# Mirrored row blocks of 16 instead of 32 in a linear-attention and Fourier-mixing kernel, with a new written-out order of work

## The chip, the cores and the metric

The kernel runs on one core of one Trainium2 chip. The metric is the device time of one execution in microseconds (us): 415.05, the median of 3 runs (414.36, 415.05 and 419.71). The core's engines have names in what follows: PE is the matrix engine (PEld is its weight load), DVE the vector engine, ACT the scalar engine, POOL the engine GpSimd, and SP issues transfers. POOL and ACT issue transfers too. Each engine works through its own queue strictly in the order in which the program put the instructions there, and waits at an instruction until what it needs is ready.

## The reference

```python
def phi(x):
    proj = np.einsum('bhsd,df->bhsf', x, w_phi)
    proj = proj - np.max(np.abs(proj), axis=-1, keepdims=True)
    return np.concatenate([np.exp(proj), np.exp(-proj)], axis=-1)
q_p, k_p = phi(q), phi(k)
kv = np.einsum('bhsf,bhsd->bhfd', k_p, v)
z = np.sum(k_p, axis=2)
num = np.einsum('bhsf,bhfd->bhsd', q_p, kv)
den = np.einsum('bhsf,bhf->bhs', q_p, z)[..., None] + 1e-06
x = (num / den).transpose(0, 2, 1, 3).reshape(B, S, H * D)

u = x + np.real(np.fft.fft(np.fft.fft(x, axis=1), axis=2))
un = (u - mean(u)) / np.sqrt(var(u) + 1e-06)
out = u + np.maximum(un @ w_ch1, 0.0) @ w_ch2
```

There are 8 batches, 8 heads, 576 rows and 64 columns a head, so x is 576 x 512 in each batch. The feature width of phi is 128, the hidden width of the last line 2048. All inputs and the output are float32; the kernel multiplies in bfloat16.

## The kernel before, in words

Each batch goes through four stages. (1) *Attention*: the features of k and q are projected by PE (psk L468, psq L522, psh L563), put through exp by ACT (KPp, KPn, QPHP, QPHN), their largest values are taken by DVE (MK L488, MQ L530), and v is scaled with them by POOL (VCn and VCp, L443). Then PE multiplies per head kv (L853, L857) and pn (L955), DVE combines the two halves (tg, cb, rd) and POOL writes x for two heads at a time into the tile X (L975). (2) *Mixing*: the two Fourier transforms are matrix products on folded rows. DVE folds X into R (L869 to L893, L998) and into CEO (L1007, L1053), PE multiplies with the tables SS and CS (psD L1035; L1019 in batch 0) and with CD and SD (pu L1087), and DVE adds the result to X (L1077). (3) *Normalising*: DVE measures each chunk of 128 rows (L1157, L1158), ACT writes UN (L1133), and a transpose by the transfer engines, issued by SP, makes UT (L1150). (4) *Feed-forward*: PE multiplies UT with W1 into psf (L1207, function `hidden`), ACT writes HT, PE multiplies with W2 into pso (L1224, `output(c)`; L1250 and L1270 for the rest), DVE adds into X (L1230), and `store` sends the chunk to the output.

Row n and row 576-n of a real transform mirror each other, so the 576 rows lie in X in five chunks: chunks 0 and 1 hold rows 1 to 256 in pairs (two neighbouring rows in one partition), chunks 2 and 3 the mirrored rows 320 to 575, chunk 4 the other 64. For the fold, the mirror image of a row must lie in the same partition. That is reached by blocks: before the change, rows 1 to 256 are cut into 4 blocks of 32 partitions in falling order (`193 - 64 * a`), and the mirrored chunk is read backwards within each block of 32 (`rearrange("p h (a r) -> p (h a) r", r=32)[:, :, ::-1]` in `queries`, a `stream_shuffle` with the mask 31 to 0 in `weigh_q`, and `rows_[:, ::-1, ...]` in the store). So q is loaded for rows 1 to 256 by 4 transfers, and chunks 0 and 1, which are stored together as "chunk 1", by 4 stores.

The order of the work is written out by hand in the string `PLAN`. Each letter advances one stream by one step: T, P, R and S are parts of attention, M mixing, D the fold, N normalising, U the scales, F the feed-forward, K, V and Q issue loads on POOL, A and B issue the transposes of q and k on SP, and Y is a *stir*: four matmuls without use that keep PE running in the start (L1322, psum tile `idle`). A step puts its instructions at once into the queues of all engines that it uses. The streams of several batches are interleaved, so that PE works on the feed-forward of batch b while the other engines prepare batch b+1.

Loads of k, v and q are issued by POOL (L258) among its own arithmetic; the stores and the transposes by SP, in one queue. In the last batch some stores are issued by ACT.

Of the kernel before, what the change touches and what calls it, by code (L numbers as in the profile page):

```python
# [10 lines left out]
ALU = mybir.AluOpType  # L11
AX = mybir.AxisListType
F32 = mybir.dt.float32
# [10 lines left out]
    "CYCCZYCYGGTRTTGZZGTYZWRTJTSRJGRJYSTPTSPKTTPJMJRTSSKMYMBMPTQPTPQVTMZTMQTMMTPCMMMTTMTHDYAMMYHHDHHKYYVD"  # L24
    "YDTMTMHTKZMRMSRTYMTTMNYMRVTYQNNMTNTSMNMBFFFRFFNUFNFSMFWFUNRUFQUMTPSFFMNTFPSMTFTNUPYFQMUFPPTVMFTPMTPF"
    "FMMFTTFMFAUTFMMFFMFMFMFMFFKRFPDFFTTTFFDVFFDRFTFFVDFFKTSRFQVFFFFMFFMTFRFFFFFSMTMFFMRTFFMSTMFTFNNMFMQF"
    "PTMMFTFSFMPTFFPTTPMFFFFMFSNBFMFPTQMFFAFMNPFTFMNMFFMFFMMFTTFFURMFFVFRMFFSTFFMFFMFVFTTPFFFFRFPDFFFTPFF"
    "FFFVDDRFFFQFDTMTFFQTSMKFFFMFFFKMRMFTTTMMFNNFFMMFMQFMFFSSMTFMTFFFNFSTPPMFTFMBFPTFPAMFFFMFNTFKMMFFFNFM"
    "FMFFMFFUMQMFFVMFFFTTPFFFFMTFFRFTTFFVFFFRFFRFDFFFFDFDFFDPTFMFTTFFFFMKFRFTMSFMRFFMFTSPMFNTMPQNSFFFFQMM"
    "MMTTTFFBMSFFFFTPMTFSFFMFFMTPVMFFFFMTPNFFNNMMMFFMAFFFMUFMFKMFFFMFFTTDTTFRFFSFFFFRVFFTMFFFFFRPTFFDFFFD"  # L30
    "RFFFTDFMFVKTPFFFFFMTMBQMFFRSFMFTSTSTMMKFFFNNSFMMFMMFTFMFPTMKFFFFPTPMTFFMFFFNMFTPPMFFFTNFQMNMVFFMFQMF"
    "MFFMUFFMFFVMAFFFFTTTTFDRFRFFTFSFFFFMRFFQFFFDFFTFFFDFFRFVDFTFMFFTTMFFMFFMFRSMFQTTTMFTQFNFMSVFFMFFTNPM"
    "MFMSTPMTFFFFSMTPPMFTFFMPPFBAFMFPFMFNNFMMVFMFMFFFMTTFRMNUFFFFFMRFFFMFFFSTFFMFFPTFFTFFFDDFFFRFTFFFDFDV"
    "RFFFMFTTFFMFMTMFRFFSMFFSFMTTNTFFMFNMMFFFMMFTFMPSTFNFFFPTFMFFTMPFFFFMPSPMFFTMFFPFTMNFFFNMFMFFFUMFMFMF"
    "FFFMFFMFMFFFFFDFFDFFFFFDFFFDFMFFFMFMFFMMFFMFNFMNFFFFFFMFFFFFMNFFFMFFNFFFFFFFFFFFFFFFNUFFFFFFFFFFFFFF"
# [5 lines left out]
def kernel(  # L41
# [74 lines left out]
    rc, rs = gc[:, 0:C], ga[:, 3 * NK:4 * NK]  # L116
    pc = const.tile([128, 5], F32, name="pc")
# [25 lines left out]
    def count_first():  # L143
        for a in range(4):
            count(pc[32 * a:32 * a + 32, 0:2], [[1, 2]], 193 - 64 * a, 2)
        count(pc[:, 2:3], [[1, 1]], 256, 1)
        nc.gpsimd.memset(pc[0:1, 2:3], 0.0)
        for j in range(2):
            count(
                rs[:, 128 * j:128 * j + 128].rearrange("p (a r) -> p a r", r=32),  # L150
                [[-64, 4], [2, 32]], 193 + j, 0,
            )
# [21 lines left out]
    def constants(b):  # L174
        nc.vector.tensor_scalar_mul(out=pn[:, 0:3], in0=pc[:, 0:3], scalar1=1.0 / S)
# [91 lines left out]
    def make_q(b):  # L267
# [138 lines left out]
    def features(b):  # L406
# [195 lines left out]
    def first_features():  # L602
# [21 lines left out]
        def project(ps, t, outer, last):  # L624
            for x, pr in enumerate((0, 3) if outer else (1, 2)):
                for jj in range(2):
                    rr = slice(64 * jj, 64 * jj + 64)
                    rq = (QT01, QT23)[t][rr, 2 * pr:2 * pr + 2, :]
                    rq = rq.rearrange("p h (a r) -> p h a r", r=32)
# [25 lines left out]
        def negative(t, outer):  # L655
            ps = pj.tile([128, 2, 4, 128], F32, tag="pj", name="psn")
            project(ps, t, outer, False)
            m = rows_of_m[outer][:].rearrange("p (a r) -> p a r", r=32)
# [521 lines left out]
    def store(b, U, c):  # L1180
        if c == 1:
            for a in range(4):
                queue = nc.scalar if b == B - 1 and a % 2 else nc.sync
                queue.dma_start(
                    out=out[b, 193 - 64 * a:257 - 64 * a, :].rearrange("(r j) n -> r j n", j=2),
                    in_=U[32 * a:32 * a + 32, 0:2, 0:C],
                )
        elif c in (2, 3):
            rows_ = out[b, 320:576, :].rearrange("(a r j) n -> a r j n", r=32, j=2)
# [201 lines left out]
```

## Time and profile before

| what | value |
|---|---|
| runs | 414.36, 415.05, 419.71 us |
| the profiled execution: its own time, its span | 415.15 us, 413.4 us |
| granted PE clock, mean | 0.995 |
| busy PE, PEld, DVE, ACT, POOL | 394.6, 259.5, 319.4, 303.8, 215.1 us |
| transferred | 42.71 MB |
| chain that ended last, by engine | PE 69%, DVE 13%, DMA 8%, ACT 4%, POOL 3%, issue 2% |
| largest parts of that chain | psf L1207 29%, pso L1224 19%, UT transposes 4% |

The span runs from the first to the last instruction. A row of the profile in order of time gives start, length, engine, line, operation, what is written and what is read, how many instructions were merged, and in brackets how long the engine stood idle before it and what ended that. A row such as "A L1 <- B L2: 2.8, 4, 1.3" in the list of waits says that A at line 1 waited for B at line 2 for 2.8 us in all, 4 times, at most 1.3. A row "580/605/1346" gives the shortest, the median and the longest duration in ns. A length in such rows includes the time in a pipeline, so two PE rows may overlap.

### The profile page before, as it was taken

What the parts mean: (1) busy time and instruction counts of PE and PEld (TensorE: products, weight loads), DVE (VectorE), ACT (ScalarE), POOL (GpSimd) and SP (SyncE); (2) the same over time, 40 slices, a digit from 0 to 9 for tenths busy, and PEclk for the clock granted to TensorE, in tenths of its full rate; (3) what the DMA queues carried; (4) which work ended last, traced back from release to release, by engine and by line L of the source; (5) the groups of instructions that cost most, each with busy time, mean ns of one, the idle gap of its engine ahead of it and who ended that gap; (6) DMA issues with size and microseconds to landing.
All of it is one profiled execution on the core that took longest, in us unless ns stands there. A gap on an engine that the chain in (4) does not pass through costs nothing.

```text
span 413.4 us, 10526 instructions
## 1 busy us (share of the span) xinstructions
PE 394.6 (95%) x4194; PEld 259.5 (63%) x4194; DVE 319.4 (77%) x662; ACT 303.8 (73%) x617; POOL 215.1 (52%) x279
## 2 busy tenths in 40 slices
PE   7898999989999989999899999999999999999994
PEld 3574577535856568566756577566856586658563
DVE  5979887999699867797689878888799768875101
ACT  6988999658958886688868886789758885544350
POOL 8997695774466753707658373649271343201000
PEclk9999899999999999999999999999999999999999
DMA  7999979898674899654965979757952141106103
GB/s 210 221 170 158 181 100 185 87 118 128 102 118 58 67 179 141 63 92 83 129 97 65 156 104 142 80 72 116 117 97 52 46 83 21 27 14 114 24 23 90
DMA packets 108520, 42.71 MB, mean 103 GB/s; under 512 B 82615, under 2 KB 103479, under 8 KB 108471
## 3 DMA queue, kind: packets, MB, share of 16 engines
q0 software_dynamic: 46272, 16.60, 37.1%
q1 hardware_dynamic: 61703, 24.85, 32.9%
q10 hardware_dynamic: 496, 0.59, 0.6%
q8 instruction: 33, 0.54, 0.5%
q14 instruction: 16, 0.13, 0.1%
HBM read 36.77 MB, written 9.44 MB: 112 GB/s over the span
## 4 chain that ended last, share of the span: by engine, by line
PE 69%; DVE 13%; DMA 8%; ACT 4%; POOL 3%; issue 2%; DVEq 0%; POOLq 0%; SPq 0%; ACTq 0%
PE psf L1207 29%; PE pso L1224 19%; DMA UT<-UN 4%; PE kv L853 3%; PE psD L1035 2%; PE psk L468 2%; DMA KT<-KS 2%; PE pu L1087 2%; DMA KS<-in_k_dram 2%; PE psq L522 2%; PE psh L563 1%; DVE MK L488 1%; PE pso L1250 1%; DVE cb L969 1%; DVE X L1077 1%
## 5 line engine op out<-in xcount | busy, mean ns | idle before, releaser
L1207 PE MATMUL psf<-UT,W1b 128*128 128x320 bf16 (+1 forms) x1024 | 141.1, 286 | 2.9 <-DMA UT<-UN 2.8
L1224 PE MATMUL pso<-W2b,HT 128*128 128x512 bf16 x496 | 120.5, 379 | 0.0
L1207 PEld LDWEIGHTS <-W1b 128*128 128x128 bf16 x1024 | 94.6, 98 | 30.9 <-issue 3.8
L1212 ACT ACTIVATE HT<-psf 128x320 bf16<-128x320 f32 x128 | 53.9, 444 | 25.7 <-PE psf L1207 19.5
L1224 PEld LDWEIGHTS <-HT 128*128 128x128 bf16 x496 | 45.2, 98 | 43.2 <-issue 0.4
L975 POOL TENSOR_TENSOR X<-cb,rd 128x640 f32<-128x640 f32 x28 | 35.1, 1254 | 52.9 <-DVE rd L973 29.6
L443 POOL TENSOR_TENSOR VCn<-VS,VCn 128x512 bf16<-128x512 bf16 x28 | 29.9, 1067 | 43.4 <-ACT VCn L438 36.6
L530 DVE TENSOR_REDUCE MQ<-psq 128x8 f32<-128x1024 f32 (+1 forms) x32 | 34.3, 1088 | 17.8 <-PE psq L522 17.4
L1230 DVE SCALAR_TENSOR_TENSOR X<-pso,rs,X 128x512 f32<-128x512 f32 x31 | 23.0, 743 | 28.2 <-PE pso L1224 28.0
L1214 ACT ACTIVATE HT<-psf 128x512 bf16<-128x512 f32 x64 | 37.3, 602 | 6.8 <-PE psf L1207 6.6
L488 DVE TENSOR_REDUCE MK<-psk 128x8 f32<-128x1024 f32 x28 | 33.8, 1210 | 1.4 <-ACT KPn L474 1.4
L474 ACT ACTIVATE KPp<-psk 128x1024 bf16<-128x1024 f32 x28 | 28.8, 1027 | 7.8 <-PE psk L468 7.5
L258 POOL DMA_DIRECT2D QS<-in_q_dram x49 | 33.4, 688 | 1.1 <-issue 1.1
L1133 ACT ACTIVATE UN<-X,MV 128x512 bf16<-128x512 f32 (+1 forms) x35 | 25.2, 726 | 11.5 <-DVE MV L1158 8.0
L572 ACT ACTIVATE QPHP<-psh 128x1024 bf16<-128x1024 f32 x28 | 28.9, 1031 | 4.8 <-PE psh L563 4.5
L474 ACT ACTIVATE KPn<-psk 128x1024 bf16<-128x1024 f32 x28 | 28.7, 1025 | 1.7 <-DVE MK L488 1.6
L443 POOL TENSOR_TENSOR VCp<-VS,VCp 128x512 bf16<-128x512 bf16 x28 | 29.9, 1067 | 0.0
L572 ACT ACTIVATE QPHN<-psh 128x1024 bf16<-128x1024 f32 x28 | 29.0, 1036 | 0.0
L1157 DVE BATCH_NORM_STATS2 st<-X 128x6 f32<-128x512 f32 (+1 forms) x40 | 27.1, 678 | 0.2
L1077 DVE TENSOR_TENSOR X<-pu,X 128x512 f32<-128x512 f32 (+3 forms) x49 | 23.5, 526 | 4.6 <-PE pu L1087 4.5
L955 PEld LDWEIGHTS <-QPHP 128*128 128x128 bf16 x280 | 20.5, 99 | 7.8 <-DVE cb L969 3.8
L1173 POOL TENSOR_TENSOR rs<-VE,mhalf 128x5 f32<-128x5 f32 (+1 forms) x9 | 10.3, 1148 | 24.8 <-DVE VE L1172 24.7
(462 smaller groups left out, 797.2 us busy)
## 6 DMA issues: line engine op xcount, KB each, us to landing
out_dram<-X SPq DMA_DIRECT2D x31, 128.0 KB
out_dram<-X SPq DMA_DIRECT2D x15, 256.0 KB
KS<-in_k_dram POOLq DMA_DIRECT2D x7, 512.0 KB, 8.2
VS<-in_v_dram POOLq DMA_DIRECT2D x14, 256.0 KB, 4.8
W1b<-in_moe_w_ch_dram POOLq DMA_DIRECT2D x1, 2048.0 KB, 15.3
W2b<-in_moe_w_ch_dram POOLq DMA_DIRECT2D x1, 2048.0 KB, 16.1
QS<-in_q_dram POOLq DMA_DIRECT2D x28, 64.0 KB, 3.6
QS<-in_q_dram POOLq DMA_DIRECT2D x7, 256.0 KB, 5.6
```

The source lines that it names most:

```text
L258: nc.gpsimd.dma_start(out=pieces[i][0], in_=pieces[i][1])
L443: nc.gpsimd.tensor_tensor(out=VC[:, hs, :, 0:D], in0=values[b][0][:, hs, :].rearrange("p h (j d) -> p h j d", d=D), in1=VC[:, hs, :, D:D + ...
L474: nc.scalar.activation(out=KP[:, hs, :, :].rearrange("p e (jp jj) f -> p jj (e jp) f", jj=2), in_=psk[:], func=AT.Exp, scale=sgn,)
L488: nc.vector.tensor_reduce(out=MK[:, 2 * pr:2 * pr + 2, :].rearrange("p e (jp jj) -> p jj (e jp)", jj=2), in_=tiles[pr][:], axis=AX.X, op=A ...
L530: nc.vector.tensor_reduce(out=o, in_=i[:], axis=AX.X, op=ALU.max, apply_absolute_value=True)
L572: nc.scalar.activation(out=o, in_=psh[:], func=AT.Exp, scale=sgn)
L975: nc.gpsimd.tensor_tensor(out=X[:, :, at:at + 2 * D].rearrange("p c (e d) -> p e c d", e=2), in0=cb[:, :, :, 0:D], in1=rd[:].to_broadcast( ...
L1077: nc.vector.tensor_tensor(out=to, in0=more, in1=to, op=ALU.add)
L1207: nc.tensor.matmul(ps, lhsT=W1b[:, cc, 128 * hh:128 * hh + 128], rhs=UT[:, cc, lo:hi], start=(cc == 0), stop=(cc == NCC - 1),)
L1212: nc.scalar.activation(out=HT[:, hh, lo:hi], in_=ps, func=AT.Relu, scale=-1.0)
L1214: nc.scalar.activation(out=HT[:, hh - 1:hh + 1, lo:hi], in_=psw[:].rearrange("p (a n) -> p a n", a=2), func=AT.Relu, scale=-1.0,)
L1224: nc.tensor.matmul(po[:], lhsT=HT[:, hh, at:at + 128], rhs=W2b[:, hh, :], start=(hh == 0), stop=(hh == NHH - 1),)
```

## The change

The blocks have 16 partitions instead of 32. So the q rows 1 to 256 of batches 1 to 7 are loaded by 8 transfers instead of 4, each half as large (the profile lists 64 KB for one of the 4), the stores of chunk 1 are 8 instead of 4, and the stores of the mirrored chunks have 8 blocks of 16 rows instead of 4 of 32. The backward reads work in blocks of 16, and the shuffle mask becomes `i ^ 15`. The tables of row numbers are made another way: two iotas fewer on POOL, three tiny steps more on DVE (a shift, a cast and a multiply-add). `PLAN` is another string: the same 1237 steps in another order. The matmuls, exponentials and reductions are the same in number and size. Most lines of the changed kernel have numbers that are 10 higher.

```diff
 PLAN = (
-    "CYCCZYCYGGTRTTGZZGTYZWRTJTSRJGRJYSTPTSPKTTPJMJRTSSKMYMBMPTQPTPQVTMZTMQTMMTPCMMMTTMTHDYAMMYHHDHHKYYVD"
+    "CZYGGTCGGCZRZZTCTWTJKSRYTPRJTSZTGYPJTSRPTJZRYMKMTSTYSJVPPTTPTQMMMTTQMMQVCTMPMMTBMTMTDKMHMYDHHHYYYYAD"
...
     def count_first():
-        for a in range(4):
-            count(pc[32 * a:32 * a + 32, 0:2], [[1, 2]], 193 - 64 * a, 2)
+        count(pc_i[:, 0:1], [[1, 1]], 0, 1)
+        count(pc[:, 0:2], [[1, 2]], 225, 2)
...
     def constants(b):
+        nc.vector.tensor_single_scalar(
+            out=pc_i[:, 1:2], in_=pc_i[:, 0:1], scalar=4, op=ALU.arith_shift_right
+        )
+        nc.vector.tensor_copy(out=blk[:], in_=pc_i[:, 1:2])
+        nc.vector.scalar_tensor_tensor(
+            out=pc[:, 0:2], in0=blk[:].to_broadcast([128, 2]), scalar=-64.0,
+            in1=pc[:, 0:2], op0=ALU.mult, op1=ALU.add,
+        )
...
-            (QS[:], q[b, :, at:at + 64 * n, :].rearrange("h (p j) d -> p h (j d)", j=2))
+            (QS[:], q[b, :, at:at + 32 * n, :].rearrange("h (p j) d -> p h (j d)", j=2))
             for QS, at, n in [
-                (QS01[32 * a:32 * a + 32], 193 - 64 * a, 1) for a in range(4)
-            ] + [(QS23, 320, 4)]
+                (QS01[16 * a:16 * a + 16], 225 - 32 * a, 1) for a in range(8)
+            ] + [(QS23, 320, 8)]
...
-                out=mq[:, hs, 2:4], in_=mq[:, hs, 2:4], mask=list(range(31, -1, -1))
+                out=mq[:, hs, 2:4], in_=mq[:, hs, 2:4], mask=[i ^ 15 for i in range(32)]
...
-                    rq = rq.rearrange("p h (a r) -> p (h a) r", r=32)[:, :, ::-1]
+                    rq = rq.rearrange("p h (a r) -> p (h a) r", r=16)[:, :, ::-1]
...
     def store(b, U, c):
         if c == 1:
-            for a in range(4):
+            for a in range(8):
                 queue = nc.scalar if b == B - 1 and a % 2 else nc.sync
                 queue.dma_start(
-                    out=out[b, 193 - 64 * a:257 - 64 * a, :].rearrange("(r j) n -> r j n", j=2),
-                    in_=U[32 * a:32 * a + 32, 0:2, 0:C],
+                    out=out[b, 225 - 32 * a:257 - 32 * a, :].rearrange("(r j) n -> r j n", j=2),
+                    in_=U[16 * a:16 * a + 16, 0:2, 0:C],
                 )
         elif c in (2, 3):
-            rows_ = out[b, 320:576, :].rearrange("(a r j) n -> a r j n", r=32, j=2)
+            rows_ = out[b, 320:576, :].rearrange("(a r j) n -> a r j n", r=16, j=2)
             nc.sync.dma_start(out=rows_[:, ::-1, 3 - c, :], in_=U[:, c, 0:C])
...
-        for which in ((0, 1, 2, 3), (4,), (5, 6)):
+        for which in (range(8), (8,), (9, 10)):
```

Three places show how the instructions move. The first is SP's queue at the boundary to batch 3: the store of chunk 2 (L1190), the stores of chunk 1 (L1184), the transposes of UT (L1150), and the stores of chunk 4 (L1193, L1194). Before:

```order
L1190 DMA out_dram<-X 4x32x512
L1184 DMA out_dram<-X 64x1x512 x4
L1150 DMA_TRANSPOSE UT<-UN 128x4x128 x2
L1190 DMA out_dram<-X 4x32x512
L1150 DMA_TRANSPOSE UT<-UN 128x4x128
L1193 DMA out_dram<-X 63x512
L1194 DMA out_dram<-X 1x512
```

and with the change:

```order
L1200 DMA out_dram<-X 8x16x512
L1194 DMA out_dram<-X 32x1x512 x8
L1160 DMA_TRANSPOSE UT<-UN 128x4x128 x2
L1200 DMA out_dram<-X 8x16x512
L1203 DMA out_dram<-X 63x512
L1204 DMA out_dram<-X 1x512
```

Eight stores instead of four stand ahead of the first two UT transposes; the third transpose has moved behind the stores of chunk 4.

The second place is DVE's queue in batch 1, from the last reciprocal of attention (rd) into the fold of X (L869) and its next steps; MK and MQ are maxima for batch 2. Before:

```order
L973 RECIPROCAL rd<-cb 128x10
L483 TENSOR_REDUCE MK_1467<-ps_1475 128x4
L530 TENSOR_REDUCE MQ_109<-psq 128x2x4
L869 TENSOR_TENSOR R<-X 128x2x2x128 x2
L869 TENSOR_TENSOR R<-X 128x2x256 x2
L875 TENSOR_TENSOR R<-X 128x255
L878 TENSOR_TENSOR R<-X 128x1
L875 TENSOR_TENSOR R<-X 128x255
L878 TENSOR_TENSOR R<-X 128x1
L488 TENSOR_REDUCE MK<-psk 128x2x4
L1230 SCALAR_TENSOR_TENSOR X<-pso,rs_1139,X 128x512
L886 TENSOR_TENSOR R<-R 128x2x255 x2
```

and with the change:

```order
L879 TENSOR_TENSOR R<-X 128x2x2x128 x2
L1182 TENSOR_SCALAR VE_1597<-MV_111 128x5
L972 TENSOR_TENSOR tg<-pn__1611,E_850 128x325
L979 TENSOR_TENSOR cb<-pn__1611,tg 128x325
L983 RECIPROCAL rd<-cb 128x10
L493 TENSOR_REDUCE MK_1399<-ps_1600 128x4
L498 TENSOR_REDUCE MK<-psk 128x2x4
L879 TENSOR_TENSOR R<-X 128x2x256 x2
L885 TENSOR_TENSOR R<-X 128x255
L888 TENSOR_TENSOR R<-X 128x1
L885 TENSOR_TENSOR R<-X 128x255
L888 TENSOR_TENSOR R<-X 128x1
```

The first half of the fold now stands ahead of the last pair of heads, and the MQ reduction has left this stretch; MK has moved ahead of the fold's second half. From L886 (now L896) to the finished CEO the same steps follow in both, with an MK and an L1230 in other places.

The third place is POOL's queue in batch 4, where it writes X for four pairs of heads (L975) among loads (L258) and products (L428). Before:

```order
L258 DMA VS_3742<-in_v_dram 64x4x64 x2
L975 TENSOR_TENSOR X<-cb,rd 128x2x5x64 x2
L1173 TENSOR_TENSOR rs_3936<-VE_3937,mhalf 128x5
L258 DMA KS_3961<-in_k_dram 64x8x64
L975 TENSOR_TENSOR X<-cb,rd 128x2x5x64
L428 TENSOR_TENSOR V4N<-VS_3742,V4N 64x4x64 x2
L428 TENSOR_TENSOR V4P<-VS_3742,V4P 64x4x64 x2
L258 DMA VS<-in_v_dram 128x4x256
L975 TENSOR_TENSOR X<-cb,rd 128x2x5x64
```

and with the change:

```order
L985 TENSOR_TENSOR X<-cb,rd 128x2x5x64 x2
L1183 TENSOR_TENSOR rs_3956<-VE_3957,mhalf 128x5
L985 TENSOR_TENSOR X<-cb,rd 128x2x5x64 x2
L268 DMA VS<-in_v_dram 128x4x256
L268 DMA QS_4128<-in_q_dram 16x8x128 x8
L268 DMA VS<-in_v_dram 128x4x256
L268 DMA KS_4246<-in_k_dram 64x8x64
L268 DMA KS<-in_k_dram 128x8x256
L268 DMA QS_4129<-in_q_dram 128x8x128
```

All four X steps now come before the loads, the eight q pieces among them.

In the start, POOL issues the large K load of batch 1 ahead of the last four VC products of batch 0 instead of behind them, and fills HI, DT and ET earlier; on PE, a stir of four matmuls that stood between the two psD groups of batch 0 now stands elsewhere; on DVE, the MK reductions that stood among batch 0's CEO and DT steps follow them. In the last batch, the eight stores of chunk 1 are issued by SP and ACT in turn, four each.

More of the change, by code (lines that the diff above doesn't have):

```diff
@@ L116 @@
     rc, rs = gc[:, 0:C], ga[:, 3 * NK:4 * NK]
+    pc_i = const.tile([128, 2], I32, name="pc_i")
+    blk = const.tile([128, 1], F32, name="blk")
     pc = const.tile([128, 5], F32, name="pc")
@@ L149, in count_first @@
             count(
-                rs[:, 128 * j:128 * j + 128].rearrange("p (a r) -> p a r", r=32),
-                [[-64, 4], [2, 32]], 193 + j, 0,
+                rs[:, 128 * j:128 * j + 128].rearrange("p (a r) -> p a r", r=16),
+                [[-32, 8], [2, 16]], 225 + j, 0,
             )
@@ L1265, in forward @@
             return
-        rows_ = out[b, 320:576, :].rearrange("(a r j) n -> a r j n", r=32, j=2)
+        rows_ = out[b, 320:576, :].rearrange("(a r j) n -> a r j n", r=16, j=2)
         for queue, at in ((nc.scalar, 0), (nc.sync, 256)):
```

26 lines of the change are left out of this document (13 added, 13 removed).

## The prediction

> **What bounds the kernel now.** I read the page's sums first, then the busy time of the stretch between the first hidden matmul (psf, L1207) at 50.90 and the last matmul's end at 407.50, then the list of PE's own waits, and last the lines in order of time at the places where PE waited.
>
> ```profile
> span 413.4 us, 10526 instructions
> PE 394.6 (95%) x4194; PEld 259.5 (63%) x4194; DVE 319.4 (77%) x662; ACT 303.8 (73%) x617; POOL 215.1 (52%) x279
> 50.90:407.50 356.60, 350.51 (x3702) 233.72 (x3701) 276.69 (x561) 259.45 (x534) 172.08 (x204) 1.00 0.66 92
> ```
>
> The third row's columns after the length are PE, PEld, DVE, ACT, POOL, the clock, the DMA share and GB/s. In this long middle PE is busy 350.5 of 356.6 us at clock 1.00, and the change leaves its 4194 matmuls as they are. So only three things can move: the 50.9 us of start, the roughly 6 us in which PE stood still, and the 5.9 us of tail (413.4 less 407.5). PE's waits in the middle are few:
>
> ```profile
> PE psf L1207 <- DMA UT<-UN: 2.8, 4, 1.3
> PE psD L1035 <- DVE CEO L1007: 1.2, 1, 1.2
> PE pn__4073 L955 <- DVE MK L488: 0.7, 1, 0.7
> PE psD L1035 <- DVE CEO L1053: 0.4, 1, 0.4
> ```
>
> **UT, the term against the change.** At each batch boundary PE waits for the first two UT transposes, and SP must issue the stores of chunk 1 just ahead of them. Batches 2 to 5:
>
> ```profile
> 142.10 2.94 SPq L1184 DMA_DIRECT2D out_dram<-X  x4
> 145.40 2.81 SPq L1150 DMA_TRANSPOSE UT<-UN  x2
> 151.88 1.03 PE L1207 MATMUL psf<-UT,W1b 128*128 128x256 bf16 x8 [1.09 <-DMA UT<-UN]
> 187.86 2.57 SPq L1184 DMA_DIRECT2D out_dram<-X  x4
> 191.77 3.52 SPq L1150 DMA_TRANSPOSE UT<-UN  x2
> 198.48 1.47 PE L1207 MATMUL psf<-UT,W1b 128*128 128x256 bf16 x12 [1.28 <-DMA UT<-UN]
> 235.93 2.58 SPq L1184 DMA_DIRECT2D out_dram<-X  x4
> 239.23 2.53 SPq L1150 DMA_TRANSPOSE UT<-UN  x2
> 244.96 1.05 PE L1207 MATMUL psf<-UT,W1b 128*128 128x256 bf16 x8 [0.23 <-DMA UT<-UN]
> 280.94 2.58 SPq L1184 DMA_DIRECT2D out_dram<-X  x4
> 284.89 2.94 SPq L1150 DMA_TRANSPOSE UT<-UN  x2
> 290.76 1.48 PE L1207 MATMUL psf<-UT,W1b 128*128 128x256 bf16 x12 [0.25 <-DMA UT<-UN]
> L1184 SPq DMA_DIRECT2D out_dram<-X x30: 580/605/1346, 94.7 to 403.6; - x30
> 382.98 6.91 PE pso L1224 x32
> ```
>
> The stores end at 145.04, 190.43, 238.51 and 283.52, so the transposes start 0.36, 1.34, 0.72 and 1.37 us behind them: there is that much room. Four stores more, at some 0.65 us each, are +2.6 us of SP per boundary. Without any move that would be late by 2.2, 1.3, 1.9 and 1.2 us. But the new order moves output(1), which releases the stores, away from the next batch's first psf. I counted the matmuls between the two in both PE orders, each at its interval (pso, the largest part, 6.91/32 = 0.216 us; the others by their own): 9.2, 10.2, 9.4 and 10.1 us before, 10.7, 11.2, 10.9 and 11.2 us now. So the stores come 1.5, 1.0, 1.5 and 1.1 us earlier, and by this path the transposes are 2.6 less that less the room: 0.74, 0.26, 0.38 and 0.13 us later. The waits would be 1.83, 1.54, 0.61 and 0.38. The other path, X to UN to UT, starts at the first pu; from there to psf PE has 8.3, 7.9, 8.6 and 9.2 us of work before and 8.0, 8.9, 8.5 and 8.4 now, which makes the waits 1.39, 0.28, 0.33 and 1.05. By the later of the two paths they sum to 5.0 us, by the second alone to 3.05, against 2.85 now: +0.2 to +2.2, I take the middle, **+1.2 us**. The lower bound is -2.85 (no wait left); the upper is the first rival below.
>
> **CEO of batch 1.** Here VectorE is the one that is late:
>
> ```profile
> 77.12 0.22 DVE L973 RECIPROCAL rd<-cb 128x10 f32<-128x10 f32 x1
> 77.80 1.22 DVE L530 TENSOR_REDUCE MQ<-psq 128x8 f32<-128x1024 f32 x1
> 78.93 2.49 DVE L869 TENSOR_TENSOR R<-X 128x512 f32<-128x512 f32 x4
> 91.19 1.88 DVE L1007 TENSOR_TENSOR CEO<-R 128x381 bf16<-128x381 f32 x2
> 93.00 1.03 DVE L1053 CAST CEO<-R 128x6 bf16<-128x6 f32 x1
> 93.13 0.55 PE L1035 MATMUL psD<-CS,CEO 128*128 128x289 bf16 x3 [1.15 <-DVE CEO L1007]
> ```
>
> From the last reciprocal to the finished CEO pass 16.9 us. The new DVE order (second pair of fences in the section on the change) takes out of this stretch the MQ reduction (about 1.13, to the next start) and moves the first half of the fold, half of 2.49, ahead of the reciprocal: 2.4 us less. By my count PE has 15.3 us of work from the last pn to this psD instead of 15.6, so CEO gains 2.1 us on a wait of 1.15, and 0.4 more for L1053: 1.55. I take **-1.4 us**; bounds -1.55 and, if more of DVE's steps are stretched as L1053 is here (1.03 us; 0.17 in its row of batch 0, below), +1.5.
>
> **MK of batch 4.** PE's wait of 0.7 us at pn__4073 comes from a DVE queue that had waited for an X step on POOL, and there a K load stood between the X steps. In the new POOL order (third pair of fences) all four X steps of this batch come before the loads, and so in most batches. **-0.7 us**, bounds -0.7 and +0.7 (as long again at another batch).
>
> **Start.** POOL issues batch 1's K load only after its last VC product, and PE runs a stir ahead of the second psD:
>
> ```profile
> 26.34 0.93 POOL L258 DMA_DIRECT2D KS<-in_k_dram  x1
> 31.87 1.04 POOL L248 MEMSET HI<- 128x512 bf16 x2
> 42.50 1.64 PE L1322 MATMUL idle<-ones_b 128*128 128x512 bf16 x4
> 43.97 0.91 PE L1019 MATMUL psD<-CS,CEO 128*128 128x289 bf16 x6
> 42.76 0.17 DVE L1053 CAST CEO<-R 128x6 bf16<-128x6 f32 x1
> 49.19 0.58 ACT L1148 COPY UT<-put 128x512 bf16<-128x512 bf16 x1
> ```
>
> Now the K load (0.93), the HI fills (1.04) and the DT/ET fills (about 0.4) stand ahead of the last four VC products, some 2.4 us. Part of it, by my reading 0.7, falls where POOL would wait for ACT anyway. So the last VC comes 1.7 us later, the first pn, which PE queues behind it, about 0.9, and the DVE chain about 0.7 later. Against that, psD no longer stands behind the stir: CEO was ready at 42.93, psD started at 43.97, 1.04 us, and two MK reductions move behind the casts. By DVE's path psf would start 1.4 us earlier, but ACT's queue, with the same products to make up to the UT copy that ends at 49.77, starts 0.7 later and leaves no more than **-0.4 us**. Bounds -1.5 (ACT follows too) and +1.7 (all of VC's delay). The three new tiny DVE steps for the row numbers and the two iotas saved on POOL cancel within 0.1 us.
>
> **What is hidden, and what the order costs PE.** The q loads take four more issues for each of 7 batches:
>
> ```profile
> L258 POOL DMA_DIRECT2D QS<-in_q_dram x49: 552/596/962, 27.3 to 282.3; - x49
> L563 PE MATMUL psh<-QT,wphi x56: 372/386/388, 56.4 to 341.0; 64*128 64x512 bf16 x56
> 122.62 1.02 PE L1224 MATMUL pso<-W2b,HT 128*128 128x512 bf16 x4
> 123.58 0.40 PE L468 MATMUL psk<-wphi,KT 64*128 64x128 bf16 x8
> ```
>
> That is 28 x 0.596 = 17 us of POOL, which stands idle 413.4 - 215.1 = 198 us; if that cover were gone, 17 us would come on top. The reversed reads of q in blocks of 16 cost nothing: of the 56 matmuls half read straight and half backwards in blocks of 32, and all take 372 to 388 ns. Four pso of 0.216 are 0.86 us, yet the psk that follows starts 0.96 us behind the first: changing from full-array to half-array matmuls costs 0.1 us. The new order has 85 such changes and the old 77: **+0.8 us**, bounds 0 and 1.
>
> **Tail.** The last batch's stores now are four on ACT and four on SP:
>
> ```profile
> 402.92 2.04 ACTq L1184 DMA_DIRECT2D out_dram<-X  x2
> 406.31 0.65 ACTq L1280 DMA_DIRECT2D out_dram<-X  x1
> 408.05 0.59 SPq L1280 DMA_DIRECT2D out_dram<-X  x1
> ```
>
> Two more on ACT, 2.04 us, push its last store from 406.31 to 408.4, done at 409.0 where SP's last one was issued by 408.64: 0 to +0.4 us, I take **0**, since a smaller last store should leave faster.
>
> **Sum:** +1.2 - 1.4 - 0.7 - 0.4 + 0.8 + 0 = -0.5 us. The profiled run took 415.15 us (its span and 1.75 us around it), 0.1 above the median of 415.05; so **414.6 us**. A measurement of this kernel can tell about 2% from no change, that is below 406.8 or above 423.4.
>
> **Rivals.** *The stores push UT at every boundary (slower).* In the tail, with two queues issuing, a store took 1.02 us on ACT (2.04 for two), and SP issued beside it. At that price eight take 8.2 us instead of 2.6, and after the 1.3 us of earlier output(1) and 0.95 us of room 3.4 us remain at six boundaries, +20 us. It decides from 0.78 us a store, where eight take 6.2 us and the loss is 1.4 us a boundary; near there the time is 424 us. For it: 2.94/4 = 0.74 in batch 2. Against it: the median of 0.605. Chance 0.1. *The new order removes nearly all waits (faster):* -2.85 - 1.55 - 0.7 - 1.5 + 0.8 = -5.8 gives 409 us. For it: the X steps stand together on POOL and output(1) is earlier everywhere; against it: the distance from pu to psf did not grow. Chance 0.2. *POOL's 17 us fall on DVE or on VC:* single DVE steps were stretched in batch 1 (L1053 by 0.86 us), and if the extra issues on POOL bring about 0.5 us of this or of late VC products to PE in each of 7 batches, +3.5: 418 us. For it: POOL stands on the path at the start; against it: PE waited for POOL in no row of the list. Chance 0.17. *A wider store:* the stores of chunks 2 and 3 go from 4 blocks to 8, and if the transfer time of the last one halves, the 4.76 us between its issue at 408.64 and the end shrink by perhaps 0.6: 414.0 us, chance 0.1. On this the Trainium skill, page "DMA: Bandwidth & Descriptors", section "Why a DMA increments its semaphore by 16 and not by 1", says that a DMA runs on the largest number of engines up to 16 that divides the slowest dimension of both sides, so 4 before and 8 now; at the page's 27 GiB/s an engine 128 KB would take an estimated 1.1 us and then 0.6. The trace of before has no landing time for stores, so no row bears it out yet. My forecast, gains and losses cancelling, has 0.43.
>
> **Range and chances.** The lower bounds of UT, CEO, MK and the start, with the 0.8 for PE's changes, give 409; the upper ones without the first rival would give 422.6 if all fell together, which I cut to 421. The range is 409 to 421, with the first rival and the far end of the second outside. Faster by over 2% takes a third of the second rival (0.07), slower most of the first and a bit of the third (0.1), the rest, 0.83, stays within 2%.
>
> **What would show it.** In the new profile: first psf near 50.5 us; no wait of psD for CEO in batch 1; waits of psf for UT of 3 to 5 us in all; POOL busy near 232 us; chunk 1's eight stores in 5.2 us. PE waiting over 1.4 us for UT at each boundary would make the first rival right; a first psf beyond 52.5, or DVE waits in the list of PE's waits at several batches, would make me wrong by the start or by the third.

## The result, and the profile after

The changed kernel took 426.79 us, the median of 4 runs (425.98, 426.16, 427.42, 427.74), beside 415.11 for the kernel before. The ratio is 1.0258 with a 95% interval of 1.0212 to 1.0304: slower by over 2%, where 414.6 us and no change had been forecast. The profiled execution took 425.98 us, and its span of 424.2 us is 10.8 longer than before. First the page's sums, then the busy time of the same long middle as before, from the first psf (L1217 now; lines after the tables stand 10 further down) to the end of the last matmul:

```profile
span 424.2 us, 10609 instructions
PE 397.1 (94%) x4194; PEld 263.8 (62%) x4194; DVE 323.6 (76%) x665; ACT 303.8 (72%) x617; POOL 226.8 (53%) x305
```

```profile
59.75:418.96 359.21, 353.47 (x3711) 237.10 (x3709) 272.87 (x559) 259.54 (x533) 182.48 (x227) 0.99 0.66 93
```

The first psf starts at 59.75 instead of 50.90: 8.85 us of the loss arise in the start. The middle is 359.21 instead of 356.60 us, 2.6 more. The tail behind it is 5.24 instead of 5.9, 0.65 less. PE's own waits name the places:

```profile
PE pt L711 <- DVE m L709: 4.7, 1, 4.7
PE psf L1217 <- DMA UT<-UN: 4.4, 4, 3.2
PE pst L355 <- DMA HT<-in_k_dram: 3.4, 1, 3.4
PE psD L1029 <- DVE CEO L1017: 2.3, 2, 1.2
PE put L1152 <- ACT UN L1137: 1.5, 1, 1.5
```

All but the psf row lie in the start. CEO of batch 1 and MK of batch 4, which PE waited for before, are no longer in the list. The 4.7 us stand behind a chain of five tiny DVE steps, which split the maxima of q into three bfloat16 parts (m, ml) so that PE can transpose them (pt). In order of time, DVE, then POOL, then PE:

```profile
22.90 1.13 DVE L706 CAST m<-MQ 128x20 bf16<-128x20 f32 x1
24.07 4.98 DVE L707 TENSOR_TENSOR ml<-MQ,m 128x20 f32<-128x20 f32 x1
29.08 0.17 DVE L708 CAST m<-ml 128x20 bf16<-128x20 f32 x1
...
23.95 0.93 POOL L268 DMA_DIRECT2D KS<-in_k_dram  x1
24.90 1.07 POOL L845 TENSOR_TENSOR VCn<-HT,VCn 128x512 bf16<-128x512 f32 x1
25.92 1.07 POOL L845 TENSOR_TENSOR VCp<-HT,VCp 128x512 bf16<-128x512 f32 x1
26.93 1.06 POOL L845 TENSOR_TENSOR VCn<-HT,VCn 128x512 bf16<-128x512 f32 x1
27.95 1.05 POOL L845 TENSOR_TENSOR VCp<-HT,VCp 128x512 bf16<-128x512 f32 x1
28.95 1.29 POOL L268 DMA_DIRECT2D VS<-in_v_dram  x2
...
29.52 0.34 PE L711 MATMUL pt<-ident_b,m 128*96 128x128 bf16 x1 [4.69 <-DVE m L709]
```

A subtraction of 128x20 elements lasts 4.98 us and ends at 29.05, where POOL's run of four VC products ends (27.95 + 1.05 = 29.00). In the kernel before the same chain had just missed this:

```profile
25.65 0.77 DVE L696 CAST m<-MQ 128x20 bf16<-128x20 f32 x1
26.46 0.18 DVE L697 TENSOR_TENSOR ml<-MQ,m 128x20 f32<-128x20 f32 x1
...
25.33 1.05 POOL L835 TENSOR_TENSOR VCp<-HT,VCp 128x512 bf16<-128x512 f32 x1
```

The last VC product ends at 26.38. The cast, which takes 0.17 us in the changed kernel at 29.08, lasts 0.77 us here and ends at 26.42, and the subtraction behind it takes its 0.18 us.

What PE lost beyond its waits shows in the granted clock. The five stretches: the 3.5 us behind the wait for pt, the next 3.5, the stop at the boundary after batch 0, the 3.5 us behind that and the 2.2 us that follow (the clock is the number ahead of the last two):

```profile
29.50:33.00 3.50, 3.48 (x37) 2.28 (x38) 1.99 (x4) 1.55 (x3) 3.50 (x8) 0.51 1.20 121
33.00:36.50 3.50, 3.50 (x80) 2.80 (x81) 2.46 (x7) 3.06 (x10) 3.50 (x6) 1.00 1.83 164
112.78:116.02 3.24, 0.00 (x0) 0.00 (x1) 0.71 (x2) 0.80 (x2) 2.54 (x5) 0.82 1.27 200
116.00:119.50 3.50, 3.48 (x18) 2.49 (x19) 0.00 (x0) 1.51 (x2) 1.62 (x3) 0.50 1.18 144
119.50:121.70 2.20, 2.20 (x25) 1.39 (x23) 0.00 (x0) 0.92 (x3) 0.00 (x0) 0.50 0.04 8
```

Behind the first of these stops PE does 3.4 us of work at half its clock, behind the second 5.7 us (3.48 and 2.20). At the full clock the same work would take half as long, so the estimated cost on top of the stops is 1.7 and 2.8 us. In the middle of the kernel before the mean clock was 1.00.

### The profile page after: what moved, and what is told of

The parts are those of the page before. It is cut to its first block, busy times and chain, and to the rows that moved or that the text cites. A ratio compares the mean times of both kernels' runs of the same rounds, so it can differ in the third digit from the quotient of the medians.

```text
span 424.2 us, 10609 instructions
## 1 busy us (share of the span) xinstructions
PE 397.1 (94%) x4194; PEld 263.8 (62%) x4194; DVE 323.6 (76%) x665; ACT 303.8 (72%) x617; POOL 226.8 (53%) x305
## 4 chain that ended last, share of the span: by engine, by line
PE 76%; DVE 11%; ACT 5%; DMA 4%; issue 2%; POOL 1%; SPq 0%; DVEq 0%; POOLq 0%; ACTq 0%
PE psf L1217 29%; PE pso L1234 20%; PE kv L863 3%; DMA UT<-UN 3%; PE psD L1045 2%; PE pso L1260 2%; PE pu L1097 2%; PE idle L1332 2%; PE psh L573 2%; PE psk L478 2%; PE psq L532 1%; DVE X L1087 1%; DVE cb L979 1%; DMA HT<-in_k_dram 1%; DVE ml L707 1%
## 5 line engine op out<-in xcount | busy, mean ns | idle before, releaser
L1217 PE MATMUL psf<-UT,W1b 128*128 128x320 bf16 (+1 forms) x1024 | 142.4, 289 | 4.6 <-DMA UT<-UN 4.4
L1234 PE MATMUL pso<-W2b,HT 128*128 128x512 bf16 x496 | 119.0, 379 | 0.0
L1217 PEld LDWEIGHTS <-W1b 128*128 128x128 bf16 x1024 | 95.9, 99 | 32.3 <-DMA UT<-UN 3.8
L268 POOL DMA_DIRECT2D QS<-in_q_dram x77 | 46.2, 614 | 9.7 <-DMA VS<-in_v_dram 5.1
L1224 ACT ACTIVATE HT<-psf 128x512 bf16<-128x512 f32 x64 | 38.2, 607 | 16.5 <-PE psf L1217 16.3
L1087 DVE TENSOR_TENSOR X<-pu,X 128x512 f32<-128x512 f32 (+3 forms) x49 | 23.4, 526 | 11.1 <-PE pu L1097 11.1
L438 POOL TENSOR_TENSOR V4N<-VS,V4N 64x256 bf16<-64x256 bf16 x14 | 8.7, 619 | 30.0 <-ACT V4N L434 29.4
```

What stands on the lines that cost most here:

```text
L268: nc.gpsimd.dma_start(out=pieces[i][0], in_=pieces[i][1])
L1087: nc.vector.tensor_tensor(out=to, in0=more, in1=to, op=ALU.add)
L1217: nc.tensor.matmul(ps, lhsT=W1b[:, cc, 128 * hh:128 * hh + 128], rhs=UT[:, cc, lo:hi], start=(cc == 0), stop=(cc == NCC - 1),)
L1224: nc.scalar.activation(out=HT[:, hh - 1:hh + 1, lo:hi], in_=psw[:].rearrange("p (a n) -> p a n", a=2), func=AT.Relu, scale=-1.0,)
L1234: nc.tensor.matmul(po[:], lhsT=HT[:, hh, at:at + 128], rhs=W2b[:, hh, :], start=(hh == 0), stop=(hh == NHH - 1),)
```

## The experiments

The theory: the loss comes from the new order's start, above all from the held subtraction. The rival: the smaller pieces make it, through the issues of loads on POOL and stores on SP. Each time is a median; ratios are to the kernel before, measured beside it on the same chip.

### Order and pieces apart

OLD and NEW are the two PLAN strings. *order_alone* is the kernel before with NEW, *pieces_alone* the changed kernel with OLD, *old_start* and *new_start* the changed kernel with the two orders joined at the first feed-forward step (written short; the kernels hold the joined string):

```diff
-PLAN = NEW
+PLAN = OLD[:140] + NEW without these steps     (old_start)
+PLAN = NEW[:136] + OLD without these steps     (new_start)
```

order_alone: 

> The kernel before with blocks of 32 (4 q pieces, 4 stores of chunk 1), run in the order of the changed kernel: the 1237 steps of the new order, nothing else. Theory A (the loss of 11 us is the new order's start: in the changed kernel's trace a 128x20 subtraction on VectorE, which takes 0.18 us elsewhere, lasts 4.98 us beside a run of GpSimd multiplications and TensorE waits 4.69 us behind it; the rest of the start is 4 us later by the order itself): 422 to 427 us, with the first psf near 59 to 60 us and a long subtraction of over 3 us. Rival B (the eight pieces and eight stores cost the time, through 17 us more of GpSimd issues and 2.6 us more of SyncE per boundary): 413 to 417 us, first psf near 51 us.

pieces_alone: 

> The changed kernel's code (blocks of 16, 8 q pieces, 8 stores of chunk 1, 8 blocks in the other stores) run in the order of the kernel before. Theory A (the order makes the loss): 414 to 418 us, first psf within 1 us of 50.9, the second and later boundaries 0 to 1.5 us longer where the stores stand ahead of the UT transposes. Rival B (the pieces make it): 423 to 428 us.

old_start: 

> The changed kernel with the old order up to the first feed-forward matmul (the first 140 steps of the kernel before), and then what is left of the new order in its own sequence. Theory A (about 9 of the 11 us arise before the first psf): 415 to 418 us, first psf near 51 us. Rival C (the later boundaries make it, and the late start would have been made up): 422 to 427 us.

new_start: 

> The changed kernel with the new order up to the first feed-forward matmul (136 steps), and then what is left of the old order. Theory A: 422 to 426 us, first psf near 60 us with the long subtraction. Rival C: 414 to 418 us.

With *old_start_32*, told further down, six combinations stand beside the kernel before:

| start | rest | blocks | kernel | us | ratio (95%) | first psf |
|---|---|---|---|---|---|---|
| old | old | 32 | before | 415.11 | 1 | 50.90 |
| old | old | 16 | pieces_alone | 423.48 | 1.0159 (1.0084 to 1.0235) | 50.39 |
| old | new | 16 | old_start | 416.97 | 0.9989 (0.9948 to 1.003) | 50.66 |
| old | new | 32 | old_start_32 | 416.26 | 1.0023 (0.9991 to 1.0055) | 50.90 |
| new | new | 32 | order_alone | 427.13 | 1.0232 (1.0148 to 1.0315) | 62.52 |
| new | new | 16 | after | 426.79 | 1.0258 (1.0212 to 1.0304) | 59.75 |
| new | old | 16 | new_start | 436.32 | 1.0451 (1.0355 to 1.0547) | 63.70 |

These runs come from different chips, so the kernel before beside each is taken off first: it took 417.35 us beside order_alone and old_start and 415.58 beside old_start_32. By these differences the new start costs 9.78 - 0.68 = 9.1 us with blocks of 32 and 11.68 + 0.38 = 12.1 with blocks of 16; the plain medians would give 10.9 and 9.8. The held subtraction (4.97 to 4.98 us) is in every kernel of the table with the new start and in none with the old. That part of the theory held.

But the rival is half right as well: in the old order the pieces cost 423.48 - 417.35 = 6.1 us (417.35 was the kernel before on that chip), which I had not expected in pieces_alone (414 to 418). new_start missed its 422 to 426 by ten: its waits for UT are 11.7 us instead of the changed kernel's 4.4, and its first psf is 3.95 us later than there. order_alone's first psf also missed, at 62.52 instead of 59 to 60. The first 136 steps are the same in the three kernels, but the clock is not: read in windows of 0.25 us, PE did 3.4 us of work at half clock ahead of the first psf in the changed kernel, 11.1 in order_alone and 9.9 in new_start. So part of what the new start costs is not fixed by its order.

In the rest of the new order the pieces cost nothing that can be measured (416.97 and 416.26). So, by these runs, the new order's rest pays for the pieces, and its start loses the time.

### The held subtraction

*s_later* moves two steps of POOL's VC products behind the V loads. The diff is the first PLAN line (cut):

```diff
-    "CZYGGTCGGCZRZZTCTWTJKSRYTPRJTSZTGYPJTSRPTJZRYMKMTSTYSJVPPTTPTQ...
+    "CZYGGTCGGCZRZZTCTWTJKSRYTPRJTSZTGYPJTSRPTJZRYMKMTTYJVSSPPTTPTQ...
```

> The changed kernel with two of its 1237 steps moved: the last two pairs of GpSimd multiplications VC <- HT,VC of batch 0 (four ops of 1.06 us, which ran at 24.9 to 29.0 us) come after the loads of V for batch 1 instead of around them. Theory A (the 128x20 subtraction on VectorE lasts 4.98 us because GpSimd's four multiplications hold something that it needs): the subtraction is back at 0.2 us, the first transposed pt at about 25 us instead of 29.5, first psf 4 to 5 us earlier than 59.8, and 421 to 423 us. Rival D (the subtraction only waited out of sight for data or for a place, or something else in the new start is late too): the first psf stays within 1 us of 59.8 and the time at 425 to 427 us.

*port_free* leaves the order alone and takes one SBUF operand away from each subtraction (the lines that only follow from it are left out):

```diff
-            left = small.tile([128, 2, 10], F32, tag="ml", name="ml")
...
-            nc.vector.tensor_copy(out=hi, in_=m)
-            nc.vector.tensor_tensor(out=left[:], in0=m, in1=hi, op=ALU.subtract)
-            nc.vector.tensor_copy(out=mid, in_=left[:])
-            nc.vector.tensor_tensor(out=lo, in0=left[:], in1=mid, op=ALU.subtract)
-            pt = pk.tile([96, 128], F32, tag="pk", name="pt")
+            pt = pk.tile([128, 512], F32, tag="pk", name="pt")
+            raw = pt[:, 256:276].rearrange("p (x n) -> p x n", x=2)
+            left = pt[:, 288:308].rearrange("p (x n) -> p x n", x=2)
+            nc.vector.tensor_copy(out=raw, in_=m)
+            nc.vector.tensor_copy(out=hi, in_=raw)
+            nc.vector.tensor_tensor(out=left, in0=raw, in1=hi, op=ALU.subtract)
+            nc.vector.tensor_copy(out=mid, in_=left)
+            nc.vector.tensor_tensor(out=lo, in0=left, in1=mid, op=ALU.subtract)
...
-            nc.vector.tensor_copy(out=mt_[:], in_=pt[:])
+            nc.vector.tensor_copy(out=mt_[:], in_=pt[0:96, 0:128])
```

> The changed kernel in its own order, with the five small VectorE ops between the maxima of batch 0 and their transpose rewritten so that none reads two operands from SBUF: the maxima are first copied to PSUM (one op more), and the difference stays in PSUM. GpSimd's four multiplications stay where they are. Theory A in its narrow form (what is held is the way on which VectorE's second SBUF operand is read beside GpSimd's reads): no op of the five lasts over 0.5 us except the first copy, pt at about 25 to 26 us, 421 to 423 us. Rival E (GpSimd's work slows any VectorE op at that place, whatever it reads): a stall of 3 to 5 us stays in the five ops, and the time is 425 to 428 us.

*held_again* adds to port_free one subtraction that nothing uses, with both operands in SBUF:

```diff
             nc.vector.tensor_tensor(out=lo, in0=left, in1=mid, op=ALU.subtract)
+            idle = small.tile([128, 2, 10], F32, tag="ml", name="ml")
+            nc.vector.tensor_tensor(out=idle[:], in0=m, in1=hi, op=ALU.subtract)
```

> The kernel of the run that keeps the differences of the maxima in PSUM (420.4 us), with one VectorE op more that nothing uses: a 128x20 subtraction of two SBUF operands into a small idle tile, right behind the five ops, where GpSimd's four multiplications of 1.06 us are under way (24.9 to 28.9 us). Theory A (an op with two SBUF operands stays out until GpSimd's whole run of multiplications is over): this op alone lasts 3 to 4 us and ends near 28.95 us, the psn and psq matmuls behind it start about 3 us later, and the time is back at 423 to 425 us. Rival I (an op waits for the one GpSimd instruction that is under way, and slips in before the next): 0.3 to 1.1 us for the op, and 420 to 421.5 us.

The times: s_later 420.71 us (ratio 1.0113, 1.0052 to 1.0173), port_free 420.36 (1.0106, 1.0034 to 1.0179), held_again 425.35 (1.0223, 1.0151 to 1.0296; runs from 421.7, the profiled one, to 427.36). The first two lie 0.3 and 0.6 us below the expected range, the third 0.35 above. First pt at 25.18, 25.48 and 25.05 instead of 29.52, first psf at 56.71, 56.52 and 60.02. In held_again PE waits 2.85 us behind the added op, and the late first psf is back, though nothing uses the op's result. In order of time, port_free first, DVE and then POOL:

```profile
24.60 0.18 DVE L709 CAST m<-pt 128x20 bf16<-128x20 f32 x1
24.82 0.19 DVE L710 TENSOR_TENSOR pt<-pt,m 128x20 f32<-128x20 f32 x1
25.04 0.18 DVE L711 CAST m<-pt 128x20 bf16<-128x20 f32 x1
25.25 0.18 DVE L712 TENSOR_TENSOR m<-pt,m 128x20 bf16<-128x20 f32 x1
...
24.85 1.07 POOL L847 TENSOR_TENSOR VCn<-HT,VCn 128x512 bf16<-128x512 f32 x1
```

and held_again:

```profile
24.82 0.18 DVE L712 TENSOR_TENSOR m<-pt,m 128x20 bf16<-128x20 f32 x1
24.91 3.65 DVE L714 TENSOR_TENSOR ml<-MQ,m 128x20 f32<-128x20 f32 x1
28.49 0.28 DVE L720 CAST mt<-pt 96x128 bf16<-96x128 f32 x1
...
24.42 1.07 POOL L849 TENSOR_TENSOR VCn<-HT,VCn 128x512 bf16<-128x512 f32 x1
...
27.47 1.05 POOL L849 TENSOR_TENSOR VCp<-HT,VCp 128x512 bf16<-128x512 f32 x1
```

Beside the same POOL products, a subtraction with one operand in PSUM takes 0.18 or 0.19 us, and one with both in SBUF stays until the last of the four is over (27.47 + 1.05 = 28.52, the op ends at 28.56). So it is not POOL's work as such (rival E is out), and the op doesn't slip in between two products (rival I is out). On this the Trainium skill, page "SBUF — State Buffer", section "Who interferes with whom", says that a VectorE instruction with two SBUF inputs contends with a GpSimd instruction that reads SBUF, and, of the ports that the two share, that whoever issues first has them for the whole instruction while the other is blocked. The kind of op agrees. A block for one instruction does not: it was 4.98 and 3.65 us, up to the end of a run of 1.06 us products. What stays open is the beginning: in the changed kernel the op's record starts at 24.07, 0.83 us ahead of the first of the four, beside a load issue, and in s_later it began at 24.11 beside the same issue and took 0.18 us.

### Loads and stores apart

*loads8* and *stores8* split, in the kernel before and its order, only the loads or only the stores, each block of 32 into two of 16. loads8:

```diff
-                (QS01[32 * a:32 * a + 32], 193 - 64 * a, 1) for a in range(4)
-            ] + [(QS23, 320, 4)]
+                (QS01[32 * a + 16 * e:32 * a + 16 * e + 16], 193 - 64 * a + 32 * e, 1)
+                for a in range(4) for e in range(2)
+            ] + [(QS23, 320, 8)]
```

> The kernel before in its own order and layout, with only the loads of q split: each of the four 64 KB pieces as two of 32 KB, 8 instead of 4. Theory J (the 8.4 us that the blocks of 16 cost in the old order come from the stores): 415 to 417 us. Rival K (they come from the loads, through 17 us more of GpSimd issues): 420 to 424 us.

stores8:

```diff
-            for a in range(4):
+            for a in range(8):
                 queue = nc.scalar if b == B - 1 and a % 2 else nc.sync
+                at = 193 - 64 * (a // 2) + 32 * (a % 2)
                 queue.dma_start(
-                    out=out[b, 193 - 64 * a:257 - 64 * a, :].rearrange("(r j) n -> r j n", j=2),
-                    in_=U[32 * a:32 * a + 32, 0:2, 0:C],
+                    out=out[b, at:at + 32, :].rearrange("(r j) n -> r j n", j=2),
+                    in_=U[16 * a:16 * a + 16, 0:2, 0:C],
```

> The kernel before in its own order and layout, with only the stores of chunk 1 split: each of the four as two of 16 partitions, 8 instead of 4, the same rows and bytes. Theory J (SyncE issues eight of them in 5.1 us instead of 2.6, ahead of the UT transposes, and the room there was 0.4 to 1.4 us): the waits of psf for UT grow from 2.9 to 8 to 10 us in all and the time is 420 to 424 us. Rival K: 415 to 417 us.

loads8 took 415.5 us (0.9988, 0.9952 to 1.0024): the loads are free. stores8 took 429.74 (1.0345, 1.0298 to 1.0392), above the expected 420 to 424: the stores are the cost. Its size is not settled. The six runs spread from 421.31 to 431.7, the two lowest (421.31 and 426.03) alone would give 8 us instead of 13.8, and the profiled one is the lowest, with waits of 6.4 us where 8 to 10 were expected. But even the lowest is above the largest of the 19 runs of the kernel before (420.43). Why the split stores alone should cost more than all the pieces in pieces_alone is open. PE's waits for UT in stores8 and in pieces_alone, each kernel's row:

```profile
PE psf L1208 <- DMA UT<-UN: 6.4, 6, 2.0
```

```profile
PE psf L1217 <- DMA UT<-UN: 9.8, 6, 2.6
```

and the boundary in pieces_alone where it costs most:

```profile
238.24 5.12 SPq L1194 DMA_DIRECT2D out_dram<-X  x8
243.46 3.14 SPq L1160 DMA_TRANSPOSE UT<-UN  x2
...
249.69 0.50 PE L1217 MATMUL psf<-UT,W1b 128*128 128x256 bf16 x3 [2.65 <-DMA UT<-UN]
```

The stores end at 243.36 and the transposes start 0.1 us behind them: the room is used up, and psf waits 2.65 us instead of the 0.23 of before. Over all boundaries 9.8 instead of 2.8 us.

### The boundary after batch 0

In the new order this boundary alone has a long wait for UT, with eight stores (3.24 us in the changed kernel, 3.32 in old_start) and with four (3.43 in old_start_32). So here it isn't the number of the stores. In old_start, the chain of waits and the order of time:

```profile
100.17 6.54 DMA UT<-UN
106.75 3.46 PE psf L1217 x16
```

```profile
99.76 0.94 POOL L268 DMA_DIRECT2D KS<-in_k_dram  x1
```

The transfer takes 6.54 us, and POOL issues the 512 KB load of k for batch 3 beside its start. *k_early* moves that step; *old_two* keeps the whole stretch in the old order; *old_start_32* is the control with four stores, and was also to tell whether the rest of the new order is worth something alone:

```diff
-PLAN = OLD[:140] + NEW without these steps
+PLAN = old_start's PLAN, the second K step of batch 3 behind the last V step of batch 2     (k_early)
+PLAN = OLD[:390] + NEW without these steps     (old_two)
```

> The kernel with the old start and the rest of the new order (blocks of 16, 417.0 us), with one step moved: the 512 KB load of k for batch 3, issued at 99.8 us beside the UT transposes of the boundary after batch 0, goes where the old order has it, about 18 us earlier. Theory L (the UT transposes last 6.5 us there because the load shares the queues' 16 engines with them): the UT transfer is 2 to 3 us shorter, the psf wait of 3.3 us falls under 1 us, and the time is 413 to 415 us. Rival M (UT is late because the store issues ahead of it on SyncE start late or last long): wait and time as in that run, 416 to 418 us.

> The changed kernel (blocks of 16) with the old order for its first 390 steps, until half of the feed-forward work of batch 1 is done, and what is left of the new order behind it. From the lengths of the batches: old order with blocks of 16 to the first psD of batch 2 at 136.87 us, then the new order's 45.6, 44.2, 45.5, 46.5, 39.6 and 51.0 us, together 409.3 us of span and 411 us. Theory H (the new order loses a second time only at the boundary after batch 0, where its eight stores stand ahead of the UT transposes and psf waits 3.3 us, and gains 5 us in the batches after): 410 to 413 us, that boundary without a wait over 1 us. Rival (the loss there is passed on to a later boundary): 414 to 418 us.

> The kernel before (blocks of 32, 4 pieces, 4 stores of chunk 1) with its own order up to the first feed-forward matmul and what is left of the new order behind it. Built up from the lengths of the batches in the run of the new order with blocks of 32 (span 423.0 us, first psD of batch 1 at 101.86) and the old start (first psD of batch 1 at 89.6): 423.0 - 101.86 + 89.6 = 410.7 us of span, 412.5 us. Theory F (the rest of the new order is worth a few us by itself, and eight pieces cost those under it): 411 to 414 us. Rival G (the rest of the new order only pays for the pieces): 414.5 to 417 us.

k_early took 413.56 us (0.9942, 0.9904 to 0.998), in the range expected, by less of the effect than expected: the load moved only 5.8 us, to 93.97, since the V step that it was put behind is itself issued at 93.20 in this order, after the eight q loads. The transfer and the wait behind it:

```profile
99.41 5.49 DMA UT<-UN
```

```profile
104.95 1.92 PE L1217 MATMUL psf<-UT,W1b 128*128 128x256 bf16 x16 [1.78 <-DMA UT<-UN]
```

The transfer is 1.05 us shorter, the wait 1.78 instead of 3.32 (under 1 was expected), and the 16 matmuls behind it take 1.92 us instead of 3.46, because the clock no longer falls. That speaks for the load beside the transposes. But the intervals of old_start and k_early overlap, the load was moved and not removed, and in old_start_32, where it is issued at 97.54, the transfer from 99.71 took 7.36 us. What share of the 6.54 us is the load's own stays open. old_start_32 came out at 416.26: rival G was right, the rest of the new order is worth nothing without the smaller pieces, and my sum over batch lengths (412.5) missed because the stretch with this boundary was 4.5 us longer behind the old start (53.2 us from psD to psD, 48.7 in order_alone). old_two took 411.67 us, ratio 0.9891 (0.9837 to 0.9946), in the range expected, and the only kernel with the start and this boundary both in the old order:

```profile
PE psf L1217 <- DMA UT<-UN: 0.7, 3, 0.3
```

It has blocks of 16, the old order for the start and the first boundary, the new order behind that. It is 3.9 us faster than the kernel before beside it, and faster than the changed kernel; it was assembled from the losses found above.

## Why the prediction was wrong, step by step

**Start: the step that failed.** "leaves no more than -0.4 us. Bounds -1.5 and +1.7" was +8.85. I priced POOL's moved steps by when their products come ready, and counted the K load, the fills and the last four products as some 2.4 us of delay for VC. What I didn't ask was what DVE does while POOL multiplies: the products moved onto the one small DVE chain that reads two SBUF operands and that PE waits for. The trace of before had a sign of it: the cast at L1053, 1.03 us instead of 0.17, which the prediction noticed, is another kind of op, with one operand, but it ends at 94.03, where a VC product of POOL ends (92.63 + 1.36 = 93.99).

With the hold taken away the first psD comes at 44.42 (s_later) or 44.22 us (port_free) instead of 49.57, 5.15 or 5.35 us earlier. Of this 3.0 or 3.2 us are left at the first psf. The stretch between the two, in before, port_free and the changed kernel, shows why:

```profile
40.40:50.90 10.50, 9.72 (x76) 5.18 (x72) 8.91 (x27) 10.03 (x21) 6.87 (x12) 0.84 1.31 182
44.22:56.52 12.30, 10.43 (x67) 5.03 (x68) 9.48 (x27) 10.29 (x23) 7.01 (x12) 0.72 0.60 77
49.57:59.75 10.18, 7.53 (x67) 4.06 (x68) 9.61 (x27) 10.06 (x23) 6.62 (x12) 1.00 0.24 29
```

PE waits twice for CEO (1.23 and 1.12 us) in port_free, in s_later and in the changed kernel, but only in the first two does the clock fall behind that. Taken from the kernel before beside each, the time falls by 6.6 us in s_later and 6.9 in port_free, more than the first psf gained. Behind it PE did 5.7 us of work at half clock in the changed kernel's trace, 3.4 in s_later's and none in port_free's, which fits. The other 5.6 to 5.8 us of the start are the order itself and the clock, which no run took apart. In port_free's trace, against before, the stretch up to the first pt is 25.48 instead of 22.42 us long, with a wait of 3.4 us for the first k at a place where the old order had stirs (what that wait costs was not tried), and the one from psD to psf is 1.8 us longer, with more of it at half clock. The prediction named "a first psf beyond 52.5" as what would make it wrong by the start, and so it was.

**UT: near in size by luck, not in place.** +1.2 was forecast; the waits are 4.4 instead of 2.8 us, +1.6, but 3.24 of them at the boundary after batch 0, which the sum didn't treat, and not by the number of the stores. At the four boundaries that the sum did treat, 3.05 to 5.0 us of waits were forecast and 0.3 remain. The eight stores take 5.1 to 5.8 us there and the transposes start 0.1 us behind them, as reckoned, but the data came sooner: at the first of the four psf starts without a wait 4.32 us behind the start of the transposes (164.98 - 160.66), where it was 6.48 before (151.88 - 145.40). Why the transposes were faster is not shown. The counter-case that the text worked out, "without any move that would be late by 2.2, 1.3, 1.9 and 1.2 us", 6.6 in all, is pieces_alone: the waits grow by 4.8 us at these four boundaries and by 7.0 in all. Rival 1 (424 us) was thus the result of the pieces in the old order, 423.48, though at 5.12/8 = 0.64 us a store and not at the 0.78 it asked for.

**CEO of batch 1 and MK of batch 4: right.** Both waits are gone from the list. In pieces_alone, with the old order, the wait for MK is still there (0.7 us).

**The middle as a whole: a cost missed.** PE was busy 353.47 instead of 350.51 us, with 9 matmuls more in this stretch (3711 instead of 3702). Of these 2.96 us an estimated 2.8 are the half clock behind the 3.24 us stop. The prediction charged a wait with its own length only. What remains, 0.1 us, leaves next to nothing for the +0.8 for changes between full and half array, which no run tested alone.

**q issues: right.** POOL's busy time rose by 11.7 us, to 226.8, not quite the 232 forecast, and loads8 shows that they cost nothing in the old order. Rival 3 had the right pair of engines, POOL and DVE, but the wrong cause, the issues.

**Tail: the wider store, as a rival.** From the end of the last store's issue to the end of the span it is 4.05 us instead of 4.76. Over all traces the kernels with 8 blocks in the stores of chunks 2 and 3 have 3.53 to 4.05 (9 kernels, mean 3.81), those with 4 blocks 3.81 to 5.46 (5 kernels, mean 4.62). That agrees with the 0.6 that the rival took, but no run changed this shape alone.

With the old start in its place the forecast would have stood as a number: old_start, 416.97, lies in the range of 409 to 421, but 3.32 of its 4.7 us of waits for UT are again at the boundary that the sum left out.

## What to carry to other kernels

When an order of work is moved, look at each small VectorE step with two SBUF operands that something waits for, and ask what GpSimd runs beside it: keep runs of GpSimd products away from it, or put one operand into PSUM, which cost one copy of 0.18 us here. Charge a wait of PE of about 3 us or more with some 2 to 3 us besides its own length, for the half clock behind it (1.6 to 3.2 us by the traces here), and look at the clock until it is back at 1.00, not only in the first 3.5 us. An order fitted to one set of transfer sizes need not fit another, and the two halves of an order can be worth opposite amounts: joining old and new at a batch boundary told in a few runs which half to keep.

## What the runs showed of the hardware that was not expected

A 128x20 subtraction of two SBUF operands took 0.18 us alone and 4.98 and 3.65 us beside a run of four GpSimd products of 1.06 us, ending with the last of them.

Between the first 10 us of the span and the tail, the traces of the 14 kernels have 22 stretches at half clock in all, and each lasted 3.4 or 6.8 us. PE did 3.2 to 6.4 us of work in each, so by the estimate above one cost 1.6 to 3.2 us. (In the first microseconds the clock is listed as 1.00 although four stirs take 1.89 us there and 1.04 later, so those are left out.) All nine stops of PE of 2.85 to 5.72 us led to such a stretch. Shorter stops went both ways: the one of 1.76 us in the kernel before (clock 0.54 over the 3.7 us behind it) and the one of 2.46 us in pieces_alone (0.50) did, the one of 1.78 us in k_early did not. At 2.65 us it went both ways: the stretch behind such a stop in port_free, and in pieces_alone (columns as above):

```profile
112.20:115.70 3.50, 3.49 (x44) 2.85 (x45) 0.23 (x1) 2.41 (x5) 2.19 (x3) 1.00 1.23 158
```

```profile
249.69:253.00 3.31, 3.31 (x26) 2.64 (x27) 0.00 (x0) 0.82 (x2) 0.00 (x0) 0.59 1.21 170
```

The Trainium skill, page "TensorE: Matmul & The Clock Gate", section "What's actually happening", says that the clock halves after an idle window of about 3.4 us, in a window that runs freely, and comes back after about as long a busy one. The rows agree with the half and with the 3.4 us, once or twice; the stops of 1.76, 2.46 and 2.65 us with a low clock behind them are shorter than the page's window. A stop of some 1.7 to 2.7 us had no fixed price here, which may be why some kernels spread over 6 to 10 us from run to run. The mean clocks of the runs fit that: 0.988 and 0.992 in the two faster runs of held_again and 0.982 and 0.983 in the two slower, 0.994 in the fastest of stores8 and 0.976 to 0.987 in the others. No run tested it.
